# New orders for the compute engines of an attention and gMLP kernel, and a narrower marking product

## The chip, the cores and the metric

The kernel runs on one core of a Trainium2 chip. The core has five instruction queues that matter here: TensorE (PE: matrix products; its weight loads are shown as PEld), VectorE (DVE), ScalarE (ACT), GpSimd (POOL) and SyncE (SP, which issues most DMAs). Each works through its own list of instructions strictly in order and waits on semaphores for the others. The metric is the device time of one execution in microseconds (us): the kernel before has a median of 224.09 over three runs (223.98 to 225.09).

## The reference

Two blocks in sequence, all in bf16, with S = 2048 tokens and D = 512:

```python
# block A: linear attention, 32 heads of 16
q, k, v = split(layernorm(x) @ wqkv)
phi = lambda t: where(t > 0, t + 1, exp(t)) + 1e-6
kv  = einsum('bhsd,bhse->bhde', phi(k), v)
z   = einsum('bhsd->bhd', phi(k))
h   = x + (phi(q) @ kv / (phi(q) . z)) @ wo
# block B: gMLP, 1792 = 2 x 896 hidden columns
z1, z2 = split(gelu(layernorm(h) @ w_in))
g   = w_sp @ layernorm(z2) + b_sp[:, None]    # mixes the 2048 tokens
out = h + (z1 * g) @ w_out
```

(This is a shortened form of it, in the order in which the kernel works. The layer norms have no learned scale.)

## The kernel before

Everything stays on chip between the first load and the last store. Tokens are cut into 16 tiles of 128. PSUM, where PE leaves its products, has eight banks of 512 fp32 columns.

How the program is made. The kernel's code first records operations: an operation is one or several instructions of one engine, with the tiles that it reads and writes. The recorders are short helpers, so many instructions carry the helper's line: PE products L434, ACT L453, DMAs L464 and transposing DMAs L467. Dependences follow from the tiles read and written, those of PSUM by bank. The order of the 1315 operations is not that of the code: a constant, `ORDER` (line 16), holds a packed list of their numbers, which `schedule` (L144) unpacks and deals out to the engines:

```python
ids = np.frombuffer(zlib.decompress(base64.b85decode(ORDER)), np.uint16).tolist()
self.order = {e: [o for o in self.seq if o.eng == e] for e in self.ENGS}
```

`emit` (L163) then puts in the semaphore waits that the dependences ask for. So an order that is another one changes neither what is computed nor what depends on what, but an engine that reaches an instruction too early stands there, with all that is behind it in its list.

The stages, in order of time, with the lines that they show in the profile:

- *0 to 12 us.* Token tiles x are loaded; DVE takes each tile's statistics (L543, gathered by L544), the reciprocal deviation rs is made by ACT for the first tiles (Ln, then Exp) and by POOL later (L549, L551, L556), DVE or ACT normalizes (xn, L588), and PE transposes the first tiles (L602); later ones go through transposing DMAs.
- *8 to 54 us.* PE projects K, then Q (weights wqkv, tokens xnT). phi takes an exponential on ACT (e), one DVE instruction on e (L614), and one that joins it with the product in PSUM: pk for K and pqT for Q (L619, or ACT and DVE L617). PE accumulates ct from pk and xn (L692), then combines it to kvm and m (L790, L794). Meanwhile DVE forms sums of weight tiles that Strassen's method needs later (L755; of w_in: ws, of w_sp: sa, sae, wt).
- *45 to 68 us.* For each of four groups of 512 tokens: PE makes the denominators (L824), ACT takes their logarithm (r) and from it the reciprocal (rcp), four SP DMAs spread rcp over the partitions (L815), DVE multiplies pqT with it (L840). Then PE multiplies pqT with m, four products for a token tile, and DVE adds x and evicts the sum as h (L852). ACT squares h and POOL makes its moments and the power -1/2 (L564 to L583, L575 to L579 for pairs of tiles), DVE normalizes (hn, L588), and SP transposes it by DMA (hnT).
- *66 to 139 us.* The gMLP's input product, in cells of seven Strassen products (`cell3`, L905; operands hnT and hs, weights win and ws): ACT copies between banks, DVE adds partial results (L882). gelu is applied on ACT at eviction (z, z1t). z2's norm: for even tiles ACT squares (sq) and POOL makes moments (L567 to L570) and the power (L583); for odd tiles DVE takes statistics (L952, L953) and POOL the power (L549, L551). DVE then normalizes in place (z<-z,st,rs, L588) and sums tiles (zt).
- *104 to 212 us.* The mixing product over tokens, Strassen again, some of it nested (`mix` L1067, `nested` L1042): operands z, zt, nv; weights wt, sa, nu. ACT adds the bias, DVE gates with z1.
- *172 to 219 us.* The out product, in pairs of token tiles (`mo_pair`, L1159), which use PSUM banks 6 and 7 (the last pair 3 and 4), then DVE adds h and the result is stored.

The marking product. In `mo_pair` all products but the first of each bank add onto what is in the bank. Ahead of that, columns that no starting product has touched must be written once. For bank 7 this is a product 512 columns wide ahead of the loop (L1210); in the loop a product 64 columns wide (L1217) does it for the last pair's bank 4, on columns 448 to 511, without `start`. Both products' values are of no use to the result.

Of the kernel before, what the change touches and what calls it, by code (L numbers as in the profile page):

```python
# [32 lines left out]
class _Prog:  # L33
# [219 lines left out]
def bass_sequential_preLN__linear_attn_block__mixer_gmlp__prompt_kernel(  # L253
# [24 lines left out]
    g = _Prog(nc)  # L278
# [43 lines left out]
    x = g.sbuf("x", o_x, [NT, D], BF16)  # L322
    h = g.sbuf("h", o_x, [NT, D], BF16)
# [6 lines left out]
    hnT = g.sbuf("hnT", o_pk, [KD, S], BF16)  # L330
# [4 lines left out]
    z1 = [g.sbuf(f"z1t{n}", o_xnT + slot[n] * ZR, [FH], BF16) for n in range(NT)]  # L335
# [14 lines left out]
    N4 = HT // 2 * (HW // 2) * 2  # L350
# [65 lines left out]
    def bank(b, n=512, lo=0):  # L416
        return psum[:, b, lo:lo + n]
# [5 lines left out]
    def PE(fn, reads, writes, ns, **k):  # L423
        return g.add("PE", fn, reads, writes, cost=ns, lat=165, **k)
# [372 lines left out]
    for c in range(KD):  # L797
        b = CB[1 - c % 2]
# [18 lines left out]
    for tg in range(NG):  # L817
# [12 lines left out]
        if tg not in MERGE:  # L830
# [135 lines left out]
    lo, hi = slice(0, HW), slice(HW, FH)  # L966
# [227 lines left out]
    for k in range(0, HT, 2):  # L1194
# [5 lines left out]
        if k == 0:  # L1200
# [9 lines left out]
    PE(lambda pe: pe.matmul(bank(7), lhsT=hnT[:, 0, 0:P], rhs=wout[:, 0, :], start=True, stop=True), [hnT[:, 0, 0:P], wout[:, 0, :]],  # L1210
       [bank(7)], 216)
    wout_sums()
    for c, i in enumerate(MIX[:-1]):
        X, Y = (3, 4) if i == MIX[-2] else (6, 7)
        if Y != 7:
            rest, any_, w = psum[:, Y, HW:512], zgT[MIX[0]][:, 0, :], wout[:, 0, 0:512 - HW]
            PE(lambda pe, rest=rest, any_=any_, w=w: pe.matmul(rest, lhsT=any_, rhs=w, start=False, stop=True,  # L1217
                                                               skip_group_check=True), [any_, w], [rest], 65)
        mo_pair(i, c % 2, X, Y)
# [34 lines left out]
```

## Time and profile before

| | before |
|---|---|
| median of three runs | 224.09 us (223.98 to 225.09) |
| profiled execution, span from first to last instruction | 222.3 us |
| PE busy | 216.2 us, 97% |
| DVE busy | 202.8 us, 91% |
| ACT busy | 142.8 us, 64% |
| POOL busy | 47.1 us, 21% |
| granted TensorE clock | 1.000 |

Of the profiled execution the page gives the span; its own time is not told, and the median is 1.8 us above that span. In the rows of the timeline the first number is the start in us, the second the length in us of one or (xN) several instructions together, then engine, line, operation, output and inputs by name with their shapes, and in brackets how long the engine had been idle and who released it. Instructions of one engine overlap at their ends, so the spacing of two starts is often shorter than the length shown: sixteen 512-column products in 3.61 us start some 0.216 us apart.

### The profile page before, as it was taken

The page shows a single profiled execution, that of the slowest core. Times are in us where ns is not written, and L with a number is a line of the kernel's source. Part 1 is how long each engine was busy: PE and PEld are TensorE (multiplying, and loading weights), DVE is VectorE, ACT ScalarE, POOL GpSimd, SP SyncE. Part 2 cuts the span into 40 slices and gives each one's busy share as a digit, 9 for nine tenths or more (in the row PEclk, how much of TensorE's full clock was granted, in tenths as well). Part 3 has the DMA queues.
Part 4 walks back from the last instruction along what each step waited for, and adds up shares of the span by engine and source line. Part 5 has one row for each costly group of instructions (what it writes and reads, how often), then busy time and mean ns, then how long its engine had stood idle before and what let it go on. Part 6 is the DMA issues. An engine that isn't in the chain of part 4 may idle for free.

```text
span 222.3 us, 3865 instructions
## 1 busy us (share of the span) xinstructions
PE 216.2 (97%) x1346; PEld 123.6 (56%) x1346; DVE 202.8 (91%) x472; ACT 142.8 (64%) x283; POOL 47.1 (21%) x133
## 2 busy tenths in 40 slices
PE   7799999999999999999999999999999999999995
PEld 7443444443344444444555556666676787767764
DVE  3899967899999999999989998999999989899995
ACT  5789663299889999999872546626475246732330
POOL 4334410000547554685720000000000000000000
PEclk9999999999999999999999999999999999999999
DMA  6758877928966555304993653995372205033574
GB/s 182 246 99 227 170 180 181 237 50 193 182 137 132 112 107 85 49 0 94 179 134 88 166 116 81 161 202 107 58 152 58 41 0 70 17 88 27 127 203 142
DMA packets 75026, 27.12 MB, mean 122 GB/s; under 512 B 64768, under 2 KB 75008, under 8 KB 75008
## 3 DMA queue, kind: packets, MB, share of 16 engines
q1 hardware_dynamic: 74304, 26.30, 57.0%
q10 hardware_dynamic: 704, 0.59, 0.9%
q8 instruction: 10, 0.16, 0.3%
q14 instruction: 8, 0.07, 0.1%
HBM read 6.95 MB, written 2.10 MB: 41 GB/s over the span
## 4 chain that ended last, share of the span: by engine, by line
PE 87%; DVE 4%; DMA 3%; ACT 3%; SPq 1%; issue 1%; ACTq 0%
PE psum L434 79%; PE psum L692 6%; DMA x<-in_A_x_dram 1%; SPq L815 1%; DMA r<-rcp 1%; ACT e L453 1%; DVE pqT L840 1%; DVE h L852 1%; DVE st L543 1%; DVE pk L619 1%; PE psum L602 0%; PE psum L824 0%; PE psum L714 0%; PE psum L790 0%; DVE e L614 0%
## 5 line engine op out<-in xcount | busy, mean ns | idle before, releaser
L453 ACT ACTIVATE psum<-psum 128x448 f32<-128x448 f32 (+2 forms) x76 | 31.1, 428 | 34.9 <-PE psum L434 28.6
L434 PE MATMUL psum<-z,wt 128*128 128x448 bf16 (+1 forms) x216 | 42.0, 335 | 0.1
L434 PEld LDWEIGHTS psum<-z,wt 128*128 128x128 bf16 x216 | 20.9, 98 | 14.6 <-ACT np L453 0.4
L434 PE MATMUL psum<-win,hnT 128*128 128x448 bf16 x112 | 26.4, 353 | 0.0
L453 ACT ACTIVATE e<-psum 128x1024 bf16<-128x1024 f32 (+1 forms) x18 | 16.7, 929 | 8.5 <-PE psum L434 8.5
L453 ACT ACTIVATE z1t<-psum 128x448 bf16<-128x448 f32 (+1 forms) x24 | 16.4, 691 | 7.3 <-PE psum L434 5.3
L434 PE MATMUL psum<-ws,hs 128*128 128x448 bf16 x72 | 19.2, 353 | 0.0
L434 PEld LDWEIGHTS psum<-win,hnT 128*128 128x128 bf16 x112 | 10.5, 98 | 11.0 <-ACT z1t L453 1.0
L434 PE MATMUL psum<-zt,sa 128*128 128x448 bf16 (+1 forms) x92 | 16.5, 316 | 0.0
L882 DVE TENSOR_TENSOR psum<-psum,p5z 128x448 f32<-128x448 f32 x24 | 15.0, 626 | 1.0 <-ACT z1t L453 0.8
L692 PE MATMUL psum<-pk,xn 128*128 128x512 bf16 x64 | 15.8, 379 | 0.1
L453 ACT ACTIVATE p<-psum,b 128x448 f32<-128x448 f32 x22 | 13.4, 634 | 3.6 <-DVE u L1030 1.8
L434 PE MATMUL psum<-m,pqT 128*128 128x512 bf16 x64 | 14.7, 380 | 0.9 <-DVE h L852 0.6
L434 PE MATMUL psum<-xnT,wqkv 128*128 128x512 bf16 x64 | 15.3, 379 | 0.0
L453 ACT ACTIVATE z<-psum 128x896 bf16<-128x896 f32 x16 | 15.0, 970 | 0.2 <-PE psum L434 0.2
L434 PE MATMUL psum<-wqkv,xnT 128*128 128x512 bf16 x64 | 15.0, 379 | 0.0
L1030 DVE TENSOR_TENSOR u<-psum,p 128x448 bf16<-128x448 f32 x22 | 13.6, 620 | 1.4 <-PE psum L434 1.0
L434 PE MATMUL psum<-wout,zgT 128*128 128x256 bf16 (+1 forms) x77 | 14.9, 302 | 0.0
L434 PE MATMUL psum<-nv,nu 128*128 128x224 bf16 x108 | 14.5, 259 | 0.1
L543 DVE BATCH_NORM_STATS2 st<-x 128x6 f32<-128x512 bf16 x15 | 9.8, 682 | 3.6 <-DMA x<-in_A_x_dram 3.6
L614 DVE TENSOR_SCALAR e<-e 128x1024 bf16<-128x1024 bf16 (+1 forms) x18 | 7.0, 390 | 5.6 <-ACT e L453 5.6
L434 PEld LDWEIGHTS psum<-zt,sa 128*128 128x128 bf16 x92 | 8.9, 98 | 5.3
(157 smaller groups left out, 452.2 us busy)
## 6 DMA issues: line engine op xcount, KB each, us to landing
r<-rcp SPq DMA_DIRECT2D x16, 128.0 KB, 2.7
out_dram<-h SPq DMA_DIRECT2D x15, 128.0 KB, 1.8
win<-in_B_w_in_dram SPq DMA_DIRECT2D x4, 448.0 KB, 3.8
x<-in_A_x_dram SPq DMA_DIRECT2D x6, 256.0 KB, 3.8
wqkv<-in_A_wqkv_dram SPq DMA_DIRECT2D x2, 512.0 KB, 4.9
wout<-in_B_w_out_dram SPq DMA_DIRECT2D x1, 896.0 KB, 5.1
wt<-in_B_w_sp_dram SPq DMA_TRANSPOSE x32, 4.1
wo<-in_A_wo_dram SPq DMA_DIRECT2D x1, 512.0 KB, 6.4
```

What stands on the lines that cost most here:

```text
L434: inst = pe.matmul(out_ap, lhsT=a, rhs=b, start=start and i == 0, stop=stop and i == len(pairs) - 1, **kw)
L453: return g.add("ACT", lambda ac: ac.activation(out_ap, in_ap, func, **kw), [in_ap, *extra], [out_ap] + ([accum] if accum is not None else []),
L543: dve(lambda v: v.bn_stats(s[:, 0:6], src[:, n, :]), [src[:, n, :]], [s[:, 0:6]], D)
L614: dve(lambda v: v.tensor_scalar(e, e, 1.0, EPS_PHI, op0=ALU.min, op1=ALU.add), [e], [e], w * GW, acc=4)
L619: dve(lambda v: v.scalar_tensor_tensor(dst, t, 1.0 + EPS_PHI, e, op0=ALU.add, op1=ALU.max), [t, e], [dst], w * GW, ps=True)
L692: inst = pe.matmul(bank(CB[c]), lhsT=xn[:, i, c * P:(c + 1) * P], rhs=pk[:, i, :], start=i == 0, stop=i == NT - 1)
L815: g.add("SP", lambda q: q.dma_start(dst, src_ap), [rcp[:, i:i + w, :]], [dst], cost=700, lat=2200, dma=f"r{tg}{c // 2}")
L840: dve(lambda v, q=q, r=r: v.tensor_tensor(q, q, r, ALU.mult), [q, r], [q], 2 * GW, acc=2)
L852: dve(lambda v, n=n, b=b, s=s: v.scalar_tensor_tensor(h[:, n, :], bank(b), 1.0, x[:, n, :], op0=ALU.mult, op1=ALU.add, accum_out=s[:, 0:1] ...
L882: dve(lambda v: v.tensor_tensor(half(b), half(src), p, ALU.add), [half(src), p], [half(b)], HW, ps=True)
L1030: dve(lambda v: v.tensor_tensor(u, half(b), p, ALU.add), [half(b), p], [u], HW, ps=True)
```

## The change

Two things. First, `ORDER` holds another list. The list of SP is the same as before, instruction by instruction, and so is the order of the DMAs that ACT issues. Of the other engines' operations this many stand at another place of their engine's list:

| engine | operations | at another place | farthest move |
|---|---|---|---|
| PE | 349 | 208 | 15 places |
| DVE | 456 | 380 | 94 |
| ACT | 255 | 160 | |
| POOL | 129 | 87 | |

The moves that the prediction speaks of, with the place in the engine's list before and after:

| engine | operation | before | after |
|---|---|---|---|
| DVE | statistics of x tile 2 | 4 | 2 |
| PE | tile 0's K projection and tile 1's transposes | | change places |
| DVE | statistics of an x tile at 20 us, ahead of e and pk | 44 | 41 |
| ACT | at 46 us: e, then r of the first token group | e, r | r, e |
| DVE | eviction of h, tile 1 | 93 | 90 |
| DVE | a norm of h (hn) | 110 | 107 |
| PE | products of pqT and m, two pairs at 54 to 68 us | | change places |
| DVE | a sum of w_in tiles (ws, at 46.45 us before) | 74 | 131 |
| DVE | sums of w_sp tiles (wt, wt, sa) | 129, 120, 153 | 187, 214, 223 |
| DVE | norms of z2, tiles 0 to 3 | 159, 164, 171, 169 | 141, 155, 165, 173 |
| DVE | norms of z2, tiles 4 to 7 | 176, 180, 185, 178 | 162, 170, 177, 172 |
| POOL | power of z2's tile 0 | behind tile 2's moments | ahead of them |
| POOL | power of z2's tile 4 | behind the start of tile 6's moments | ahead of it |
| ACT | squares of z2 tiles 8 and 10 | 111, 118 | 118, 122 |

Second, bank 7's marking product: the one 512 columns wide goes, and the loop's 64-column product is now made for bank 7 too, in the first turn. It reads the first tile of zgT and wout, and stands in PE's list two products ahead of the first product into bank 7.

```diff
-ORDER = "c-jrsg92EG76ibvyXVHXZM%(a+qN4!jcwbuZQHgR+kEdQX3Qd3M1#e%kQT`zTPO=_AuOClv8Wc>qF
...
+ORDER = "c-jrsg92EG76ibvyXVHXZQE&V+qP}nwr!hjY@2Ot+sS+L6BE(QA{Z>5g|d)Fi)@iBtcA0v7RAC_T
...
-    PE(lambda pe: pe.matmul(bank(7), lhsT=hnT[:, 0, 0:P], rhs=wout[:, 0, :], start=True, stop=True), [hnT[:, 0, 0:P], wout[:, 0, :]],
-       [bank(7)], 216)
     wout_sums()
     for c, i in enumerate(MIX[:-1]):
         X, Y = (3, 4) if i == MIX[-2] else (6, 7)
-        if Y != 7:
+        if c == 0 or Y != 7:
             rest, any_, w = psum[:, Y, HW:512], zgT[MIX[0]][:, 0, :], wout[:, 0, 0:512 - HW]
             PE(lambda pe, rest=rest, any_=any_, w=w: pe.matmul(rest, lhsT=any_, rhs=w, start=False, stop=True,
                                                                skip_group_check=True), [any_, w], [rest], 65)
         mo_pair(i, c % 2, X, Y)
```

More of the change, by code (lines that the diff above doesn't have):

```diff
@@ L15 @@
 SEM_NS = 45.0
-ORDER = "c-jrsg92EG76ibvyXVHXZM%(a+qN4!jcwbuZQHgR+kEdQX3Qd3M1#e%kQT`zTPO=_AuOClv8Wc>qFG!EZ()okbBk|*C9&w1z;at6OK3?grzN&zmdA2gDobv8EuW>f6jsPmS{lo5g)OZWup*Yu3R(=yVCgNU)v;n0%Q9Il%VHU=u4T5`*4FA-QLArREt|ErzpS`5vg}sU8e1D{XF05bwYPt)ft9urR?!+-U+Z8Ut&^3ps#ePSS!}Che_LlOYhA3rRkmvOuT`-D*3|}DIje3HZLl@9I5x<J*?7BQO>Brwvf)<4CRj}?Z<DQ=O|hXi&AM50n`$j=x^=giw#Zsq51VC6td%Xb#n#hi*fJYwy==LSuoZU8R@y4tWxZ{Wjk49Y+xA)?+h=QRwC%UqHpbT40Xt}iY>qv#n>N<w+F@H~M{J(WxAk_^#@PnjiUqdOHrY12ZCmY;J-3Cn-5%R9+hIHHxLvdBw%JbDe|FBE*-1NVr)-Ozw@bDS7wm<dw##<k&e#=uYCCb!Lg15qw2-)JpY4@>u$Xvfp+LN}SO7vJ3}WMp3Gt8!@$uCnBQfH@5g;ypSQ31*DEMwE@Y7NwIieyV{#a7{vT!g&M>0f1SUj)<_-!$e2Dy<6X;Bt=5FQzj5=D>>c@Y8WQ32%;5&4i2`B4-FP#*Uz5(=UYilHL1pg0PlKI$SX3Zn!{A~RYe8%iM)D&cRmLj%;qU#N^WsDhqoh#aVjYAB5@$d2}Cgg&T_GU$cjXpDc*7i}>LwU7(7(E*2%6JOB;M=$~%u?zpA6Q-dlYM?WEV>G&8CTe0oMq)aeVJXI77VcO-%)kot$1)7SYz#zm9K~2HM|XTf3yi}`%)ubs!vTE99lW<5IDxr1hOYR5L%5HY=!U!aiIZ4`*Y*&<&<dxp8jmm@$1wp1@c<KX8bk3IZ|oAD;1vdA9<uW?hG0I<U=3bl0j^*Ya_}mK;WyS|3f^EH{@^b<jc2hP<Tb3vTf`^$H?KoHhpC9mw-zuY6YvHWBPZi=GD7h`B;p2y<~xL7E+*zvB;<K4#506p628YG+(cwPM{agwQbu7KZo~&vR#--5ccx`DF2N>*V>;$xU0y(5_F#TS=VlaSc&6t?^yCY~U?F})ZD!yt6ksprV;z1%M%H5y-bQ^UV^KC>VP;})He@j-XJ+<cITmLGenulkWK8bhOEhMAreG_^;=kO^5{%8(tiUYn%bkqGHXO(=NXd%a#Z=77ww%jK?9Y-M#5gR)*&M)j+|4=c$0i)Y_8iQiT)=ru&G~G~1Kh)5T*%UF#&OKX;cU)D+=2Hj!?#?_@m$5qoWOUyYsdKyS92meup^i716%N+P2vcyVM~7GWPavueBwwRW)&{wT2^H>e&Ifh;uNmqRDS1Zp5QW0<5za#L9XXse&ZOP<PR?A3ZCKyj^!`@<VKd|5pLpdPUj)6<Z13_bwZo@hi7>1|Mc#~3{stWlr<;?a^2^7hR_y<)Ha@FD0Sg6&SYp^WIEkr6@^hvhSeor;8xycI9=v7hSw}U;uTicRX$)Ob!7xS=0ir*9$aT+)#43C(Gx~fRNdr%jIO7wqpFIfTa2M+yv>-Zr8|tRnu?>i+Q)h-sCatLgo>}6ddURJr9{fB#LB0nN}?C6uU9OpWGbeHdd&t(uHt&bluDu8YNQfMrIJdoLQ11js;wf*q|$1v!b+|3%C9CWqY65q?5e9uYN`Tip|V=4f0R)zl}ByVUagf?9aK)u)LE0&T$xovUDQ!iv|Jg~Nz>KVE2^t{sG7QIn!2l%dTN0F)=IVWHJYJp8mND~zxrvWX6d`;Xtidmx7KQ|)~THasjYr!yf$dC)@!5s=!k}>msaVh7HX(QsDp3PFm2W%4Od?s)>ci`NS)Nb+M;Eer)?Ug(ORN|`b+bbR^j}VCTN$&=(iT=tj21wj%%DIYP$|;w|1zL?^O=%R7XFppW3HCdaN_bqU##zdlcT!>4yH(Bpp*EKd)4NNf&feceFy6wO<!?Kv(tT|7G72{H}f}vR~12MfENo-DCPa(L1}my}wX2cfY2mx~*9LQh~?u2;S9WdmF#6DBjIOcz5sN!#%Et^amQ@J$=6S@)#b<M|p3L=lQ*lztX?n*ZX^X590$pu@CZop2QRQ0w3V1J)w{GAwI^3`Wub)<UZcVc`^^}6aAqkcqxCRbUw+`dm_){lf9}Z^(p>LQ$3@<)oV@nus+Rac?zH5GrfS%@wvX;7y4p<r$xTR)A)NW^_0Hcmw5*Ntd;&jJAH+x^~}D?cX%d0?`yr9XYtj3!6SMO&*|$utFQ4*UfTciY@Xe7d39gs1%0D$@W1_|F8Xf&q%FS3w|XJZ>wA5$@Aopk&$sz5Kj?-1fS2_zI^>r;pFi`XUe1quO+V#_{iN6OuR7wFy|$P4V_wH|`w6e$SG<PT^D}<d>v|C{=JoxB7xk<D+^_j{Z|uXoxZm^!-o#6K3BTbDy`nesTi)Coc?<uh+kV$8`5nLSoBf_w_A1`gANfOn;30yR{@7pnYiBUqTm3)skiiq5=W&AnJXD~dwZHK&LFnL}hYQ~NX%8C&!3Pf?y!3Pa-aUvE#0{SMM~@Ih3E~A2gD)OE_~y}qPyWLr2Qh-r9yR#s@q?JbFOL;`^#noe;JYUZ{&>RRw<iuPND}-H1t^N4"
@@ new lines @@
+ORDER = "c-jrsg92EG76ibvyXVHXZQE&V+qP}nwr!hjY@2Ot+sS+L6BE(QA{Z>5g|d)Fi)@iBtcA0v7RAC_T#IHhx4`0C5{quREvY52yq3@sSu)FG$t|(vv;3CIQdkK4%TiiuD`07?u!XjQmeyie5es7(ET$E;x)#d{Svsq2#Vx(nvpUwsGFg4gXbmijWwv%!%(7WlYiv2Ky_K@I*2EfG2g`0HtfS?yidNDZSsCkO{jHL9wk}rM%33uWXq7Ftm9t#d)w)>~8)VgOfK|1@HpIGHd8=WQY?w8(p*F?h*hs5sH?64+x2ZPSYS}a!Wz(&KHMix~(`MKRn`td<j`gsXHrIODQfp<)>>rzDt!;(vvz6A{X4@EBWqoY4t+v~?#`fA;>uZ18SX*cN?SS>O^)}At+d&&|hiro#wRv{fZrKETZVT*)O|*r!(T>?7+hjYi*f!e^``5PEL)&RvZHeu&NA}o`+itsVCv1=1ux)nI?%8%bW#{d*?ZG*FYA@`vU9gvS#;({!J8M_%nq9Jx_+%d~Cf?Zx3xUt}#A1PXW}yJYMreF7Aq?Un5#r;kMMh%8fg=gNSzHA8VNvkiQsAfkvgC-0)JTXwmK0$T9fo8GhiLe132@)iAO`Xx71E+8!XqCtpd3;n9rB|X(jy`&;x9x%0c1pZ)I~uQ!d;7m3Mh;$D2{q)fFj6>5~zfdXpd~jgi@%CTxf_ksE;bhjGQQqMre!PsEQoej>hPKYUqdTsE#tIfj(%5Q7DW4Xo9{tf~KgAv1o=oIEp%Gj*h5_6ZneU7=TXLi*eYAnHY%97>)7hf)%KRL70Ux7>qeMfFYQTmFSB9tQ%HiE>>XzzM%!?VIq2>C5GZ4j^R7j;4bFlBo1Q%j-wa;LwBsjPn^OX9Kt%BMi0EUdsvSLn1nO<fmT?EhggKxxR1#gfnRupw>AZrF$|CK3L9_*!;zgEF&$^|%B~^@Ut=V$;T(Qr6W(Adaxy-R=dlaU>sXApApam2Z{PyN8Muheh|2^7Lo(nc<YqjE;xs%#BHqM1gl1yqVF*4&LN3EIEI}A1;dA6=WWK;syhjfv<t;?vZKUA`Y(aj8WmKkRPv&DZhU33T$K?pmt*FOdjKIHGh!Gi`1(=?FxD7E_kQrEq^;wiL8Ht4%i$$1`v00bBnT*BQkS|f3eVK`kn3?67h5guoCD@q#`4O!dhsoK5yZ8wen3XA5k)M&0yP1lW*oH$mfP2`Ml{tv1*^UcXg@1D}2eK;XaUrv@8i#Wz_i{elvm_UD1c$K$5Aq+5WGOCTbx!0cF5(xI=2GrP8NTN-mgO5;%OmW_No>kH)`^|Dj>|ck%{ZA4tU0@IJzH=EPjCvyupGzoZ){)<j^lVv<y)TQN*>}yw&Z@i<20_~2d?G>PUlDN<0j7FXU=3Re&SJX=3%bk79QXiZsja~<u)GUckaVCZs&Ra;Bo%sFLvcU{^o4Hx0?Jzs5VXKSc}wIp5X=Vpp;I5y3=)+rx`-0IG2}LMIjYh7a2;I*^LhwMspZe;dF)98D3X;hxd7nRTV*zw389_4<7LbBkLv~Fq$4Sif-`<qv|Q6tA=7Img*{|p0SW_Gq(O^9R0_*dd~War`k%WYKpJ@e90F~p!`atzm!<Hl~hSoOAYjj#gt6N)lje5NXeB)CG>_Vl|p&dSS6K8rIcQ2R9Hn+T6I)ZnN&tiR6rHfRP|I=sZ~+UlwBQESuIsgC$&NyHOe!pmCCEFMteRrS0}YmR<-ql>Z%s1q-n~m)~c!M>ZZ;bs0?baRT``{+NkyFu2~wSPCnMBYmBedY<2NoYVUKERz1{CU364EwOPY-Oj|TWoqeW;tG9A#j{0bW`YM}7Xr0z-zWQmNhH9j?YP1&UghpwbW@wW7YrDp1fEMbMHffP|=(v_Br*>+bmTIw<E1WM=cptC5`l(%7t-p0x6SP}Lv`62yUq5tO|LBp<=&|-`tS0M*ChCyRDUzR64&78&Kd<P1P?7zBvS^B)=s!jE=ZfZ0{Dpq$mLm9X-BC=B<#+W*FLmMnnZMFyT~s^2r`R6HZ!48w(Iv(67!IE*d0fAytBUU(oPJ%2-TkTlRX6YMNxY+{_E6r#pDBSS^Pb+vdwD_+JdyYIwEji~yszI^8c*&IG{7I~tp<5NU*t)>zc2Q59>QO1sHgCO9@+={5KrmpJ*1EG+&;p``*44+T|U9X`XtZbOFg4c^eMi?KWnmQ^4&hwGy4~PP#DkR-!#o<cr~Byvpk>Y@ajI(=Xyk+?Q=Y<*YssR-?RC0U*H9Og|GBgp552@JFWJdp35(I9xvk`Rmk)EC$06;zQJqwCST{ne2W+My}sTrdRf2hfB9D5=tX?9|LxoTAK&5Se4p?1{eHmr_#rRq2R*OX^74MzYx`Fn@j8CYD|lT$;Ya<MSM+**%Io_jKklc!fuHm%Ud+$>RX^v&{hD9*k^bCocoQ$-H~p43^-^Ba8~Sap<juX2xA4Z^(*O0!e#igwd;Zd!c~#%$5B#n_^!r}LLj;e!mA~@WKF<*_Sm=*EWS}5U(Aq-<PrQu>!5a?~gbu<5?>ua9#^3q}_aJ<5-rxHRj~he^KKfIS5JU;$1rdWU9zFQx(SlF@!y^YVg3tcbqXzMVSivuk8GQ8wLG0kWCkp;}!r-?j4lGC#{0}I;ilG"
```

## The prediction

> **What bounds the kernel now.** I read the page from the top: span and busy times, the chain of work that ended last, then PE's waits.
>
> ```profile
> span 222.3 us, 3865 instructions
> ...
> PE 216.2 (97%) x1346; PEld 123.6 (56%) x1346; DVE 202.8 (91%) x472; ACT 142.8 (64%) x283; POOL 47.1 (21%) x133
> ...
> PE 87%; DVE 4%; DMA 3%; ACT 3%; SPq 1%; issue 1%; ACTq 0%
> ```
>
> TensorE (PE) is the bound: 97% busy, and 87% of the chain. No PE product goes but one, so a new order can win only time in which PE stands still. The waits of PE name who holds it (us in all, times, longest):
>
> ```profile
> PE psum L602 <- DVE xn L588: 1.2, 2, 0.9
> PE psum L626 <- POOL warm L471: 1.0, 1, 1.0
> PE psum L434 <- DVE h L852: 0.6, 2, 0.4
> PE psum L434 <- DVE pqT L840: 0.2, 1, 0.2
> ```
>
> It is VectorE (DVE) nearly every time. Where, the table by stage shows (stretch, length, then busy us of PE, weight loads, DVE, ACT, POOL; granted clock; DMA share; GB/s):
>
> ```profile
> 54.40:68.00 13.60, 12.76 (x60) 5.24 (x61) 12.74 (x33) 11.86 (x27) 6.45 (x22) 1.00 0.78 159
> 68.00:104.00 36.00, 35.95 (x187) 16.92 (x185) 35.91 (x87) 35.19 (x71) 22.55 (x53) 1.00 0.42 77
> ...
> 139.00:176.00 37.00, 36.94 (x268) 25.69 (x268) 35.69 (x86) 19.13 (x45) 0.00 (x0) 1.00 0.61 114
> ```
>
> The clock is full throughout. From 54 to 68 us PE stands visibly (12.76 of 13.60); from 68 to 104 DVE and ACT are as full as PE; from 139 on PE has no gap, so what is done there can only lose. An estimate of what there is to win after the first 7 us, from the spacing of PE's products against their count: 0.3 at 22, 1.7 from 54 to 68, 0.7 from 68 to 104 and 0.7 from 131 to 139, in all some 3.4 us.
>
> **The change, step by step.** SP's list, and with it every DMA's place in its queue, stays as it was, and so do the DMAs that ACT issues; the lists of PE, DVE, ACT and POOL change. "Place" is the place in an engine's list.
>
> *1. Head.* DVE takes the statistics of x tile 2 (place 4 to 2) into its wait for tile 1's data; PE does tile 0's K projection before tile 1's transposes.
>
> ```profile
> 4.50 1.29 DVE L543 BATCH_NORM_STATS2 st<-x 128x6 f32<-128x512 bf16 x2 [0.43 <-DMA x<-in_A_x_dram]
> ...
> 7.08 1.04 PE L602 MATMUL psum<-ident,xn 128*128 128x128 bf16 x12 [0.32 <-DVE xn L588]
> 7.52 0.47 SPq L464 DMA_DIRECT2D wqkv<-in_A_wqkv_dram  x1
> ...
> 12.16 0.43 PEld L434 LDWEIGHTS psum<-xnT,wqkv 128*128 128x128 bf16 x3 [0.22 <-DMA wqkv<-in_A_wqkv_dram]
> ```
>
> PE's first products come up to 0.43 + 0.32 = 0.75 us sooner. But at 12.16 the first Q projection waits for a weight whose load was issued at 7.52 behind other loads on SP, which no compute order moves. What is won before stands there again: bounds 0 and -0.75; I take -0.05, near the wait that remains.
>
> *2. At 20 us.* A statistics instruction (half of the 1.29 above, 0.64 us) goes ahead of DVE's e and pk.
>
> ```profile
> 20.44 0.46 DVE L614 TENSOR_SCALAR e<-e 128x1024 bf16<-128x1024 bf16 x1 [0.31 <-ACT e L453]
> 20.93 1.23 DVE L619 SCALAR_TENSOR_TENSOR pk<-psum,e 128x1024 bf16<-128x1024 f32 x1
> ...
> 20.19 1.90 PE L434 MATMUL psum<-wqkv,xnT 128*128 128x512 bf16 x8
> 22.21 1.04 PE L692 MATMUL psum<-pk,xn 128*128 128x512 bf16 x4
> ```
>
> DVE idles 0.31 there, so the instruction costs at most 0.64 - 0.31 = 0.33 on the chain to 22.21, and nothing if the statistics' tile allows it to start while DVE waits. It starts when pqT before it ends, near the start of that idle time: bounds 0 and +0.33, taken +0.05, since the two PE products swapped there (places 21 and 22) give PE other work meanwhile.
>
> *3. At 46 us.* ACT does the first token group's logarithm r ahead of the exponential e, which before came first.
>
> ```profile
> 46.19 1.06 ACT L453 ACTIVATE e<-psum 128x1024 bf16<-128x1024 f32 x1
> 47.10 0.72 ACT L453 ACTIVATE r<-psum,epst 128x512 f32<-128x512 f32 x1
> ...
> 47.74 1.23 DVE L619 SCALAR_TENSOR_TENSOR pqT<-psum,e 128x1024 bf16<-128x1024 f32 x1
> ...
> 49.27 1.04 PE L434 MATMUL psum<-xnT,wqkv 128*128 128x512 bf16 x4
> ...
> 51.64 1.02 ACT L453 ACTIVATE e<-psum 128x1024 bf16<-128x1024 f32 x1 [0.27 <-PE psum L434]
> ```
>
> e, DVE's e and pqT slip by 0.72; pqT ended at 48.97 and PE's product that overwrites its bank came at 49.27, a slack of 0.30. So PE waits 0.72 - 0.30, about +0.4, and nothing behind takes it back: the next e, at 51.64, waits for PE. Bounds 0 (DVE, relieved of one 0.6 us sum, still starts no sooner than e) and +0.72.
>
> *4. From 54 to 68 us.* DVE evicts tile 1's h three places sooner (93 to 90), a hidden-layer norm goes from 110 to 107, and two pairs of PE's attention-out products are swapped.
>
> ```profile
> 54.41 3.61 PE L434 MATMUL psum<-m,pqT 128*128 128x512 bf16 x16
> 58.39 1.04 PE L434 MATMUL psum<-m,pqT 128*128 128x512 bf16 x4 [0.37 <-DVE h L852]
> ...
> 62.70 3.63 PE L434 MATMUL psum<-m,pqT 128*128 128x512 bf16 x16 [0.25 <-DVE h L852]
> 61.18 3.54 SPq L815 DMA_DIRECT2D r<-rcp  x4
> 66.93 0.69 DVE L840 TENSOR_TENSOR pqT<-pqT,r 128x1024 bf16<-128x1024 bf16 x1 [0.60 <-DMA r<-rcp]
> 67.68 1.04 PE L434 MATMUL psum<-m,pqT 128*128 128x512 bf16 x4 [0.23 <-DVE pqT L840]
> ```
>
> Sixteen products from 54.41 at 0.216 each end at 57.87; the next began at 58.39, so 0.52 us were lost to the eviction, which the move covers. The stall at 62.70 (0.25) may go with the swaps. But late next is the chain at the end: four r transfers, 3.54 us of issuing that SP does in order, then the landing and DVE's multiply at 66.93, and PE waits for it. That chain begins with PE's denominators behind the product of 58.39, so it moves ahead with the 0.52 and no further. Bounds 0 and -1.4 (the stage's 1.7 less what stands before 54.41); I take -0.6, the covered stall and a little.
>
> *5. From 68 to 104 us.* Three sums are put off past this stretch (places 129 to 187, 120 to 214, 153 to 223) and one out of step 3's; the norms of z2's tiles are pulled ahead: tile 0 from place 159 to 141, tile 6 from 185 to 177; POOL does tile 0's power straight after its moments.
>
> ```profile
> 45.85 0.69 DVE L755 TENSOR_TENSOR sae<-wt 128x1024 bf16<-128x1024 bf16 x1
> 46.45 0.62 DVE L755 TENSOR_TENSOR ws<-win 128x896 bf16<-128x896 bf16 x1
> ...
> 80.83 0.31 POOL L569 TENSOR_SCALAR st<-st 128x1 f32<-128x1 f32 x1
> ...
> 93.02 0.26 POOL L567 TENSOR_SCALAR st<-st 128x1 f32<-128x1 f32 x1 [1.37 <-ACT sq L453]
> 97.21 0.89 POOL L570 TENSOR_SCALAR st<-st 128x1 f32<-128x1 f32 x1
> 98.19 0.68 POOL L583 TENSOR_TENSOR rs<-st,expo 128x1 f32<-128x1 f32 x1
> ...
> 96.93 1.08 DVE L755 TENSOR_TENSOR zt<-z 128x1792 bf16<-128x1792 bf16 x1
> 101.23 0.50 DVE L588 TENSOR_SCALAR z<-z,st,rs 128x896 bf16<-128x896 bf16 x1
> ```
>
> A sum takes 0.60 (45.85 to 46.45), so by 102 us DVE is some two sums (the third comes in exchange for a statistics pass), 1.1 us, ahead. Against it: tile 0's norm now stands some 7 us sooner, and its power can end at about 80.83 + 0.31 and two short POOL steps (0.24 and 0.64, estimated), 82.1, when DVE is there about 0.4 sooner and stands. Tile 6's norm is reached at 96.93 (eight places sooner), and its power ended at 98.87; POOL fills its 1.37 of idling before 93.02 with the steps moved there, and if the 0.89 at 97.21 takes the usual 0.24, the power ends near 98.87 - 1.37 - 0.65 = 96.9. So of the 1.1 us some 0.7 remain up to that norm, and nothing behind it; only the stage's 0.7 us of PE stalls can be bought with it, and I take half, -0.3. Bounds: -0.7, and 98.87 - 96.93 = +1.9 if POOL comes no sooner.
>
> One page bears on POOL's share of that. The row of one POOL step (times, then least, median and largest ns):
>
> ```profile
> L570 POOL TENSOR_SCALAR st<-st x10: 225/240/1065, 5.9 to 108.9; 128x1 f32<-128x1 f32 x10
> ```
>
> Nine of ten alike and one four times as long: something holds POOL at times. The Trainium skill, page "SBUF — State Buffer", section "SBUF: two separate sides", says that VectorE and GpSimd share a pair of ports, as an exclusive lock held for a whole instruction. By that rule DVE's two-input sums beside POOL's chain lengthen it as the new order happens to pair them, and the sum would go from gain to loss, as rival C works out from the row; the long one agrees with it, no run here isolates it.
>
> *6. After 104 us.* PE's, DVE's and ACT's orders change in places, among work that has no gap before (36.94 of 37.00). The put-off sums come back here, about 0.5 us of DVE more ahead late on; DVE's free 1.3 of 37 us cover it. Taken 0; bounds 0 and +0.5. The 0.7 us at 131 to 139 is a chain of sums and products whose order stays.
>
> *7. The marking product.* In the chain's rows (start, us):
>
> ```profile
> 176.12 0.21 PE psum L1210
> ...
> 212.07 0.03 PE psum L1217
> ```
>
> The wide product goes, a second narrow one comes, on the gapless part: 0.03 - 0.21 = -0.18. It reads zgT's first tile, which an output product uses some 4 us before, so no wait is added.
>
> Sum: -0.05 + 0.05 + 0.4 - 0.6 - 0.3 + 0 - 0.18 = -0.68. The profiled execution is known by its span, 222.3, which would become 221.6; 1.8 us lie between it and the median of 224.09, taken as unchanged: 223.4.
>
> **Rivals.** A, the relief carries through: step 3 stays hidden because denominators move ahead too (0), step 4 yields its whole 1.4, step 5 half: -1.4 - 0.35 - 0.18 = -1.9, 222.2. For it: DVE ends nearly every wait of PE. Against: SP's 3.54 us of issues stay in order.
>
> B, slower, POOL's powers: DVE works in order, so a norm reached before its power holds up every eviction behind it, in a stretch where DVE has 0.09 us free of 36. If tile 6's power ends at 98.87 as before, step 5 is +1.9 in place of -0.3: -0.68 + 2.2 = +1.5, 225.6. It decides where POOL gains less than the 1.1 us that DVE gains. For it: POOL began the tile's moments only when ACT's square let it (1.37). Against: the steps now ahead fill that wait.
>
> C, slower, POOL's steps stretch: two of tile 6's four steps at 1.065 in place of 0.24 add 1.65 us to its chain: -0.68 + 1.65 = +1.0, 225.1. For it the one long step, against it nine short ones. This is what the Trainium skill's rule cited in step 5 would do here.
>
> D, the order does nothing: the weight's landing, SP's r chain and the sums at 137 us are fixed, gains and losses cancel, and the marking alone remains: 223.9.
>
> **How the numbers follow.** About 0.5%, 1.1 us, is what this kernel's measurement can tell from no change. Forecast 0.40 and D 0.08 lie within it (its own range 223.0 to 224.3); A 0.26 is faster; B 0.17 and C 0.09 slower. The time is the forecast's, 223.4. The range takes in A and C and stops just short of B's 225.6: 221.9 to 225.5.
>
> **What would show it.** PE's wait for h at 58 us gone; a new PE wait of 0.4 us near 49; the last r multiply still waiting for its DMA; DVE idle before L588 of z2 by under 0.5 us; no 0.21 us product at L1210. Wrong it is if DVE stands a microsecond or more for POOL at a z2 norm, if PE gets gaps after 139 us, or if the stage from 54 to 68 loses its stalls whole.

## The result and the profile after

The changed kernel is slower: 225.72 us median (225.0 to 226.34) against 224.06 us, a ratio of 1.0061 (95% interval 1.004 to 1.0082), where 223.4 was forecast, with 221.9 to 225.5 as the range. A second measurement, on the chip of the first experiments, gave 225.33 against 224.05, 1.0062 (1.0042 to 1.0081). (The ratio is not the quotient of the two medians, which is 1.0074; the means of the runs, 225.63 and 224.28, give 1.0060.) The profiled execution took 225.64 us, with a span of 223.8, which is 1.5 longer than before.

The page and the waits of PE after the change (us in all, times, longest):

```profile
span 223.8 us, 3856 instructions
...
PE 216.4 (97%) x1346; PEld 122.9 (55%) x1346; DVE 203.7 (91%) x472; ACT 143.3 (64%) x283; POOL 48.6 (22%) x133
...
PE 72%; DMA 8%; DVE 7%; ACT 6%; POOL 3%; issue 1%; SPq 1%; ACTq 0%; POOLq 0%
```

```profile
PE psum L434 <- DVE pqT L840: 0.5, 1, 0.5
...
PE psum L434 <- DVE z L588: 0.4, 1, 0.4
PE psum L434 <- DVE psum L882: 0.3, 1, 0.3
```

PE is as busy as it was, in a longer span, and POOL, which was in no place of the chain, now holds 3% of it. The wait for h that was the largest of the attention stage is gone; behind the head two new ones have come, for z2's norm (L588) and for a partial sum in PSUM (L882). One stretch of the table by stage, before and then after (columns as in the prediction's table):

```profile
106.00:116.00 10.00, 10.00 (x55) 5.11 (x53) 9.33 (x23) 8.24 (x17) 4.79 (x12) 1.00 1.18 165
```

```profile
106.00:116.00 10.00, 9.26 (x49) 4.45 (x48) 9.43 (x22) 6.18 (x13) 5.89 (x15) 1.00 1.08 166
```

Between 106 and 116 us PE was without a gap before (10.00 of 10.00); now it stands, and gets 49 products done in place of 55.

A ledger makes this exact. PE's products follow each other at fixed spacings (512 columns 0.216 us; eight of 448 columns start to start 1.51). I summed these along each kernel's own list and took the sum from the starts: what remains is the time that PE has stood by then. The table gives, by stage, how much more or less a kernel's PE stands than that of the kernel before (us; the last stage includes the shorter marking product). The kernels below "changed" are those of the experiments, described further down; "(before +)" marks the ones made from the kernel before, the others are made from the changed kernel.

| kernel | to 26 | 26-51 | 51-72 | 72-106 | 106-116 | 116-143 | 143-end | sum |
|---|---|---|---|---|---|---|---|---|
| changed, first | +0.60 | +0.31 | -0.30 | -0.39 | +1.09 | +0.20 | -0.01 | +1.49 |
| changed, second | +0.21 | +0.32 | -0.31 | -0.40 | +1.09 | +0.20 | 0.00 | +1.11 |
| squares_back | -0.20 | +0.32 | -0.31 | 0.00 | +0.24 | +0.20 | -0.02 | +0.23 |
| square8_back | +0.02 | +0.32 | -0.31 | 0.00 | +0.24 | +0.20 | -0.02 | +0.43 |
| wt8_later | +0.43 | +0.32 | -0.31 | -0.40 | +0.74 | +0.36 | -0.01 | +1.13 |
| squares_wt8 | -0.14 | +0.32 | -0.31 | 0.00 | +0.08 | +0.36 | -0.01 | +0.29 |
| hn_back | +0.42 | +0.32 | -0.10 | -0.40 | +1.10 | +0.20 | 0.00 | +1.53 |
| exp_first | -0.51 | 0.00 | -0.38 | -0.40 | +1.09 | +0.20 | 0.00 | 0.00 |
| square8_exp | +0.63 | 0.00 | -0.03 | 0.00 | +0.24 | +0.20 | -0.01 | +1.03 |
| squares_off (before +) | +0.66 | 0.00 | -0.74 | -0.14 | +2.05 | +0.01 | +0.01 | +1.84 |
| sums_off (before +) | +1.08 | +0.22 | -0.87 | +0.40 | +0.41 | +0.36 | 0.00 | +1.59 |
| stage54_mark (before +) | +0.31 | 0.00 | +0.20 | -0.02 | 0.00 | 0.00 | -0.19 | +0.30 |
| mark_only (before +) | +0.31 | 0.00 | 0.00 | 0.00 | 0.00 | 0.00 | -0.18 | +0.13 |

The two executions of the changed kernel agree to 0.01 us in every stage but the first, where loads land, and differ there by 0.4. So a stage behind 26 us can be read to a few hundredths, and the head can not. The one great loss stands at 106 to 116 us: +1.09, twice the other losses behind the head (0.31 and 0.20), and more than the gains (0.30 and 0.39).

The square of z2's tile 8 on ACT and the start of that tile's moments on POOL, before:

```profile
95.32 1.04 ACT L453 ACTIVATE sq<-z 128x896 bf16<-128x896 bf16 x1
```

```profile
98.96 0.55 POOL L567 TENSOR_SCALAR st<-st 128x1 f32<-128x1 f32 x1
```

and after:

```profile
100.64 0.98 ACT L453 ACTIVATE sq<-z 128x896 bf16<-128x896 bf16 x1
```

```profile
101.80 0.27 POOL L567 TENSOR_SCALAR st<-st 128x1 f32<-128x1 f32 x1 [1.35 <-ACT sq L453]
```

What happens from there on, read in the chain of waits of the changed kernel (start, length in us):

```profile
100.75 0.96 ACT sq L453 x2
...
101.80 0.28 POOL st L567
102.14 0.55 POOL rs L551
...
102.78 1.44 POOL st L569
...
104.60 0.57 POOL rs L583
...
105.52 0.56 POOL rs L551
106.10 0.51 DVE z L588
...
111.47 0.59 POOL rs L551
...
113.06 0.52 DVE z L588
113.63 1.50 PE psum L434 x7
```

and in its timeline, DVE and PE:

```profile
102.43 1.08 DVE L755 TENSOR_TENSOR zt<-z 128x1792 bf16<-128x1792 bf16 x1
103.43 0.69 DVE L755 TENSOR_TENSOR wt<-wt,wt 128x1024 bf16<-128x1024 bf16 x1
...
106.10 0.51 DVE L588 TENSOR_SCALAR z<-z,st,rs 128x896 bf16<-128x896 bf16 x1 [0.29 <-POOL rs L551]
...
111.58 0.63 DVE L882 TENSOR_TENSOR psum<-psum,p5z 128x448 f32<-128x448 f32 x1
...
113.06 0.51 DVE L588 TENSOR_SCALAR z<-z,st,rs 128x896 bf16<-128x896 bf16 x1 [0.44 <-POOL rs L551]
```

```profile
112.26 0.55 PE L434 MATMUL psum<-win,hs 128*128 128x448 bf16 x2 [0.31 <-DVE psum L882]
...
113.63 1.69 PE L434 MATMUL psum<-z,wt 128*128 128x448 bf16 x8 [0.43 <-DVE z L588]
```

ACT's square of z2's tile 8, put off in the new order (start 95.32 before, 100.64 now), lets POOL begin that tile's moments only at 101.80 (98.96 before). From there POOL, which works in order, has no break until its last power ends at 113.02. The powers of odd tiles stand in the same list: tile 11's (105.52) comes right behind tile 8's (104.60), tile 15's is the last. DVE reaches the norms of these two ahead of their powers and stands 0.29 and 0.44 us, with all that is queued behind; PE waits for the partial sum and the norm that come late. That the late square is the cause is tested below.

### The profile page after: what moved, and what is told of

Its sections match the earlier page's. It is cut to its first block, busy times and chain, and to the rows that moved or that the text cites. A ratio compares the mean times of both kernels' runs of the same rounds, so it can differ in the third digit from the quotient of the medians.

```text
span 223.8 us, 3856 instructions
## 1 busy us (share of the span) xinstructions
PE 216.4 (97%) x1346; PEld 122.9 (55%) x1346; DVE 203.7 (91%) x472; ACT 143.3 (64%) x283; POOL 48.6 (22%) x133
## 4 chain that ended last, share of the span: by engine, by line
PE 72%; DMA 8%; DVE 7%; ACT 6%; POOL 3%; issue 1%; SPq 1%; ACTq 0%; POOLq 0%
PE psum L434 67%; PE psum L692 5%; DMA wqkv<-in_A_wqkv_dram 5%; DMA xnT<-xn 2%; DVE z L588 1%; DMA r<-rcp 1%; DVE st L952 1%; ACT e L453 1%; SPq L815 1%; POOL st L569 1%; ACT ct L453 1%; DVE h L852 1%; ACT z L453 1%; POOL rs L551 1%; POOL rs L583 1%
## 5 line engine op out<-in xcount | busy, mean ns | idle before, releaser
L453 ACT ACTIVATE psum<-psum 128x224 f32<-128x224 f32 (+2 forms) x76 | 31.5, 425 | 33.3 <-PE psum L434 25.1
L434 PE MATMUL psum<-z,wt 128*128 128x448 bf16 (+1 forms) x216 | 41.2, 335 | 0.6 <-DVE z L588 0.4
L434 PE MATMUL psum<-ws,hs 128*128 128x448 bf16 x72 | 18.7, 353 | 0.0
L882 DVE TENSOR_TENSOR psum<-psum,p5z 128x448 f32<-128x448 f32 x24 | 14.9, 624 | 0.3 <-ACT z1t L453 0.2
L434 PE MATMUL psum<-nv,nu 128*128 128x224 bf16 x108 | 13.8, 259 | 0.1
```

What stands on the lines that cost most here:

```text
L434: inst = pe.matmul(out_ap, lhsT=a, rhs=b, start=start and i == 0, stop=stop and i == len(pairs) - 1, **kw)
L453: return g.add("ACT", lambda ac: ac.activation(out_ap, in_ap, func, **kw), [in_ap, *extra], [out_ap] + ([accum] if accum is not None else []),
L882: dve(lambda v: v.tensor_tensor(half(b), half(src), p, ALU.add), [half(src), p], [half(b)], HW, ps=True)
```

## The experiments

**The changed kernel again.** No edit.

> The changed kernel once more, as a control on the chip of the next three. If the loss is in the order, PE has again some 1.07 us of gaps at 112 to 114 us, in front of the cell product that waits for L882 and of the mixing product that waits for the norm L588 of z2, and the time stands some 1.5 us above the kernel before. If the 0.36 us that the first Q projection came later (12.64 against 12.28) was the spread of DMA landings and not the order, that figure differs by 0.2 us or more from the first profile; if it is the order, it stays within 0.1.

The gaps of 1.09 us came back to the hundredth, at 225.33. For the head this run alone decides nothing: the first Q projection started at 12.50 in place of 12.64, and 0.14 lies between the two limits that were set. Over the fourteen profiled executions it started between 11.82 and 12.64, by 12.11 to 12.47 with the head of before and 11.82 to 12.64 with the new one. With one and the same order it spreads by 0.8 us, so the 0.36 us between the first two profiles is not shown to be the order's.

**squares_back.**

```diff
 ACT, changed kernel
   z (gelu) of tile 8, z of tile 10
+  square of tile 8
   ... four evictions of the input product's cells
-  square of tile 8
+  square of tile 10
   z1t, z, z
-  square of tile 10
```

> The changed kernel, with ACT's squares of z2 tiles 8 and 10 back at their places of before (ahead of the four evictions, and behind the last of them). Theory S (POOL starts the moments of tile 8 only at 101.80 because the square comes 5.3 us later than before, and is busy without a break from there to 113.0): POOL's step starts near 99.8, its last power ends some 1 us sooner, PE's gaps at 112 to 114 shrink from 1.07 to 0.4 or less, against up to 0.4 us of new gaps at 97 to 104 from the later evictions: 225.2. Theory W (what counts is the two DVE sums back to back, zt and wt, that hold up a POOL step for 1.43 us and delay DVE itself): the gaps stay above 0.8, 225.6.

224.54 us, 1.0023 (1.0009 to 1.0037), below the 225.2 that was expected: by the time more than half of the loss is gone with two of ACT's instructions, by the ledger behind the head about half (+0.90 to +0.43). What the two profiles differ in besides lies in the head (+0.21 and -0.20), which the edit does not touch. POOL's timeline:

```profile
100.12 0.27 POOL L567 TENSOR_SCALAR st<-st 128x1 f32<-128x1 f32 x1
...
101.10 0.30 POOL L569 TENSOR_SCALAR st<-st 128x1 f32<-128x1 f32 x1
```

The moments start at 100.12, and the step that took 1.43 us takes 0.30. The gaps at 106 to 116 fall from +1.09 to +0.24; what the put-off square had won at 72 to 106 (0.40) is given back in full. Theory S holds for the gaps.

**wt8_later**, and **squares_wt8**, which adds it to squares_back.

```diff
 DVE, changed kernel
   zt sum (102.43)
-  wt sum (103.43)
   ...
   last norm of z2 (113.06)
+  wt sum
```

> The changed kernel, with the wt sum that stands at DVE's place 187, at 103.43 us, put behind the last norm of z2, so that it no longer follows the zt sum of 1.09 us. Theory W: the POOL step L569 that took 1.43 us ends with the zt sum, so takes 0.9 or less, DVE and POOL are 0.6 us sooner at the last norms, and PE's gaps at 112 to 114 shrink from 1.07 to some 0.3: 225.0. Theory S: POOL still starts tile 8's moments at 101.8, and the gaps stay above 0.8: 225.6.

> Both edits together, the squares back and the wt sum later. If both causes add, PE's gaps at 112 to 114 are gone (under 0.2 us) and the time is 224.6 to 224.9; if one of them is the whole cause, the time equals that of the one that helps alone. If neither is, it stays at 225.7.

225.27 (1.0052), between what the two theories gave, and 224.68 (1.0024). In wt8_later the POOL step becomes shorter, as theory W has it, and ends with the sum that is left:

```profile
102.25 1.08 DVE L755 TENSOR_TENSOR zt<-z 128x1792 bf16<-128x1792 bf16 x1
```

```profile
102.59 0.91 POOL L569 TENSOR_SCALAR st<-st 128x1 f32<-128x1 f32 x1
```

1.43 us with two sums beside it, 0.91 with one, 0.30 with none. But on PE this wins 0.35 at 106 to 116, and 0.16 is lost again behind, where the sum now stands. With the squares back the same edit moves 0.16 from 106 to 116 us to the next stage (0.24 to 0.08, then 0.20 to 0.36) and wins nothing. So W is real and small.

**square8_back.** As squares_back, with tile 10's square left where the change put it.

```diff
 ACT, changed kernel
   z (gelu) of tile 8, z of tile 10
+  square of tile 8
   ... four evictions
-  square of tile 8
```

> The changed kernel, with ACT's square of z2 tile 8 alone back at its place of before; that of tile 10 stays put off. If it is tile 8's square that POOL stands for (idle 1.35 us before that tile's moments) and tile 10's finds POOL busy anyway, PE's gaps at 112 to 114 fall from 1.07 to 0.4 or less as with both back, while half of the 0.4 us won at 97 to 104 is kept: 224.3 to 224.6. If both squares count, the gaps stay above 0.6: 224.9 or more.

224.66 (1.0025, 1.0012 to 1.0038), and the ledger is that of squares_back in every stage behind the head. Tile 8's square is the whole of it, on both sides of the account: I had expected to keep half of the 0.40 won before, and none was kept.

**squares_off.** The kernel before, with nothing but the two squares put off.

```diff
 ACT, kernel before
   z of tile 8, z of tile 10
-  square of tile 8
   ... evictions, psum<-psum
-  square of tile 10
+  square of tile 8
   p5z, z1t, z, z
+  square of tile 10
```

> The kernel before, with one thing of the change alone: ACT's squares of z2 tiles 8 and 10 put off to their new neighbours (behind the four evictions, and behind the next gelu). Theory S (late squares make POOL late, and DVE stands at a z2 norm): POOL's moments of tile 8 start some 1.5 us later than their 98.96, those of tile 10 some 3 us later, PE gets gaps of 0.8 us or more at 106 to 114, against up to 0.3 us won at 97 to 104: 224.6 to 225.6. If the squares hurt only together with the new order of POOL and DVE, the gaps stay under 0.3 and the time is 223.8 to 224.1.

225.89 against 223.91, 1.0098 (1.0072 to 1.0124): above what was expected, and more than the whole change costs. POOL, DVE and PE there:

```profile
100.97 0.27 POOL L567 TENSOR_SCALAR st<-st 128x1 f32<-128x1 f32 x1 [2.20 <-ACT sq L453]
...
104.83 0.27 POOL L567 TENSOR_SCALAR st<-st 128x1 f32<-128x1 f32 x1 [3.02 <-ACT sq L453]
```

```profile
108.06 0.51 DVE L588 TENSOR_SCALAR z<-z,st,rs 128x896 bf16<-128x896 bf16 x1 [1.42 <-POOL rs L583]
```

```profile
110.29 0.55 PE L434 MATMUL psum<-ws,hs 128*128 128x448 bf16 x2 [1.38 <-DVE psum L882]
```

In the order of before POOL takes tile 8's and tile 10's moments early, so it stands 2.20 and 3.02 us for them, DVE stands 1.42 at the norm, PE 1.38 behind DVE. The late squares suffice by themselves. With the new order of POOL and DVE they cost less (1.09 in the change, 2.05 here); which of its moves does that was not tested.

**sums_off.** The kernel before, with the four DVE sums alone at their new places.

```diff
 DVE, kernel before (places)
-  74 ws,  129 wt,  120 wt,  153 sa
+ 131 ws,  187 wt,  214 wt,  221 sa
```

> The kernel before, with the four DVE sums alone (one of w_in, three of w_sp) put off to the places that they have in the changed kernel, 0.5 to 1.7 us less of DVE work ahead from 46 to 104 us. If DVE's relief buys PE's gaps from 68 to 104 us, as the prediction's step 5 has it, they fall by 0.3 from 0.7 us and the time is 223.6; if it buys nothing, the gaps stay and the time is 223.9 to 224.1; if the sums come late for the mixing products, PE has new gaps at 110 to 140 us and the time is 224.3 or more.

225.31, 1.005 (1.0034 to 1.0066). From 72 to 106 us PE stands 0.40 us longer, not less, and from 106 to 143 us 0.77 longer: the time of the third case, with a loss from 72 to 106 us that none of the three had. The first new gap of that stage, where the sum of w_in now goes ahead of the sums of hn:

```profile
79.94 0.54 PE L434 MATMUL psum<-ws,hnT 128*128 128x448 bf16 x2
80.61 0.55 PE L434 MATMUL psum<-ws,hs 128*128 128x448 bf16 x2
```

Two products of 448 columns take 0.38 us, and 0.67 passed. The w_in sum had stood at 46 us beside a DVE that waited for ACT anyway, and was moved into the stage in which DVE is full. What the three sums of w_sp do there without it was not tested.

**hn_back.** The changed kernel, with DVE's first norm of h behind two more evictions, as before.

```diff
 DVE, changed kernel
-  94 hn, tile 0
   h, h
+  96 hn, tile 0
```

> The changed kernel, with the first norm of h (hn, tile 0) at DVE's place 96 as before in place of 94, behind two more evictions of h. If DVE's stand of 0.47 us there (its power on POOL ended at 60.16) is what makes PE wait 0.69 us at 63.70 for the multiply with r, that gap shrinks to 0.3 or less: 0.4 us faster than the changed kernel, 224.9 to 225.2. If the r chain is the limit all the same, the gap stays and the time is that of the changed kernel.

225.52, 1.0068 (1.005 to 1.0086): no gain. In the changed kernel DVE stood at that norm, and PE behind the multiply:

```profile
60.20 0.41 DVE L588 TENSOR_SCALAR hn<-h,st,rs 128x512 bf16<-128x512 bf16 x1 [0.47 <-POOL rs L583]
```

```profile
63.70 2.76 PE L434 MATMUL psum<-m,pqT 128*128 128x512 bf16 x12 [0.53 <-DVE pqT L840]
```

With the norm back the first stall shrinks and another appears at the end of the r chain:

```profile
63.05 2.76 PE L434 MATMUL psum<-m,pqT 128*128 128x512 bf16 x12 [0.35 <-DVE pqT L840]
...
68.69 1.47 PE L434 MATMUL psum<-m,pqT 128*128 128x512 bf16 x6 [0.51 <-DVE pqT L840]
```

```profile
66.57 0.69 DVE L840 TENSOR_TENSOR pqT<-pqT,r 128x1024 bf16<-128x1024 bf16 x1 [0.49 <-DMA r<-rcp]
```

So with the norm back the four r transfers become the limit, which in the changed kernel they were not: there the last multiply with r, at 67.58, followed without a wait. The reason stands in SP's list, where tile 0's transposed norm (hnT) is directly ahead of these transfers. In the changed kernel and then with the norm back:

```profile
60.64 1.19 SPq L467 DMA_TRANSPOSE hnT<-hn  x1
61.87 2.88 SPq L815 DMA_DIRECT2D r<-rcp  x4
```

```profile
61.20 1.19 SPq L467 DMA_TRANSPOSE hnT<-hn  x1
62.44 3.24 SPq L815 DMA_DIRECT2D r<-rcp  x4
```

A norm that DVE does 0.57 us later holds back SP, and with it r, by the same 0.57, though rcp itself was done at 61.54.

**exp_first** (the changed kernel with ACT's e ahead of r at 46 us again) and **square8_exp** (that and square8_back).

```diff
 ACT, changed kernel, 46 us
-  r, e, rcp
+  e, r, rcp
```

> The changed kernel, with ACT's exponential e ahead of the logarithm r at 46 us, as before. If that swap is what makes PE wait 0.20 us at 50.19, the wait goes, the later r costs nothing, and the time is 0.2 to 0.3 us shorter: 225.1 to 225.4. If the sooner r was needed, the multiply with r at 54 us waits for its DMA, up to 0.4 us, and the time is that of the changed kernel or above.

> The changed kernel with tile 8's square back and the exponential e ahead of r at 46 us. If the two losses are separate, the gains add (0.8 and 0.4): 223.9 to 224.2, level with the kernel before. If the stage from 54 to 68 takes one of them back, 224.4 or more.

224.93 (1.0043, 1.0027 to 1.0058), a little under its expectation, and 224.68 (1.0017, 1.0002 to 1.0032), within the second case that was expected. The +0.31 of 26 to 51 us goes, as expected; but DVE now waits for r's transfer and PE behind it:

```profile
51.71 0.69 DVE L840 TENSOR_TENSOR pqT<-pqT,r 128x1024 bf16<-128x1024 bf16 x1 [0.26 <-DMA r<-rcp]
```

```profile
54.00 2.33 PE L434 MATMUL psum<-m,pqT 128*128 128x512 bf16 x10 [0.30 <-DVE pqT L840]
```

The stage 51 to 72 then stood at -0.38 in one and -0.03 in the other, so from 26 to 72 the swap is worth 0.39 in one and 0.04 in the other: unclear. That stage moves even where its order is the same (0 in mark_only, -0.74 in squares_off, both with the order of before there): SP took 3.45 us to issue the last four r transfers in the one and 2.64 in the other.

**stage54_mark** (the kernel before, the new order between 54 and 69 us alone, and the narrow marking product) and **mark_only** (the narrow product alone).

```diff
-    PE(lambda pe: pe.matmul(bank(7), lhsT=hnT[:, 0, 0:P], rhs=wout[:, 0, :], start=True, stop=True), ...
-        if Y != 7:
+        if c == 0 or Y != 7:
```

> The kernel before, with the changed kernel's relative order of PE, DVE, ACT and POOL between 54 and 69 us alone, and the narrow marking product. If that stage's order is the one part of the new orders that wins by itself (some 0.35 us of PE's gaps there, beside 0.16 for the marking), the time is 223.4 to 223.6, under both kernels; if the r chain takes it back, 223.8.

> The kernel before, with its order, and the narrow marking product at the place of the wide one. PE's spacing there goes from 0.216 to some 0.05 us, and as nothing else moves the time falls by 0.16 us: 223.9. If a wait shows up in its place (zgT or the bank), the fall is less than 0.1.

224.46 against 224.16 (1.0017, 1.0006 to 1.0029): above both cases that were expected; the stage's order wins nothing by itself (+0.20 in the ledger). mark_only took 223.84 against 223.91, 1.0001 (0.9982 to 1.0021): the product itself is as cheap as worked out, and the sum too small for the time to show.

```profile
176.27 0.19 PE L1215 MATMUL psum<-wout,zgT 128*128 128x64 bf16 x1
176.29 1.68 PE L434 MATMUL psum<-zt,wt 128*128 128x448 bf16 x8
```

No kernel here is faster than the kernel before beyond its interval.

## Why the prediction was wrong

Step by step, with the ledger's numbers (predicted, then measured):

- Step 1, the head: -0.05; no difference that stands out of the landing of loads, which spreads PE's standing up to 26 us from -0.51 to +1.08. Not contradicted, and the greatest noise of this kernel.
- Step 2, 20 us: +0.05; the gap at pk was 0.43 in two pieces before and 0.41 in one after. Right.
- Step 3, r ahead of e: +0.4; +0.31, with the wait where it was placed (PE at 50.19 for pqT L619). The mechanism right and the size nearly so. Whether the sooner r wins part of it back at 54 us stays unclear (exp_first and square8_exp).
- Step 4, 54 to 68 us: -0.6; -0.30. The covered stall went, but the r chain was not the limit that the step took it for. PE stood longest behind a multiply that DVE reached late (0.53 at 63.70), after 0.47 us at a norm of h that was moved from place 96 to 94 and not looked at; that norm also sets when SP comes to the r transfers (hn_back).
- Step 5, 68 to 104 us: -0.3; -0.39, right by number and wrong by reason. DVE's relief bought nothing on balance: with the squares back nothing of the 0.39 is left (squares_back), and the four sums by themselves cost 0.40 (sums_off). What won it was ACT: the put-off square let four evictions through sooner. That the number came out near is luck. The row of L570 was also misread: it gives the least, the median and the largest of ten, not nine alike. In the trace of before six of the ten take some 0.23 us, two some 0.4, one 1.065 and one the 0.89 at 97.21 that the step itself shows.
- Step 6, after 104 us: 0, with +0.5 as the upper end; +1.09 at 106 to 116, +0.20 up to 143 and +0.15 behind it (the table's -0.01 holds the marking's -0.16). **This is the step that failed.** It took the order to change "among work that has no gap before" and let DVE's free time cover it. PE had no gap there, but POOL's list had no room for a late input. The two squares of z2's tiles 8 and 10 stood in the table of moves, and I gave them no price and followed nobody who waits for them. The row that rival B quotes, POOL standing 1.37 us for a square, showed the link. They were to be followed as the z2 norms of tiles 0 to 7 were: square, moments, power, norm, product.
- Step 7, the marking: -0.18; -0.16 (0.216 before, 0.058 after with the wait at its start). Right.

The measured steps add up to +0.9 us, beside the head's spread: a slower kernel, as it came out. Tile 8's square is half of that (+0.85 at 106 to 116, -0.40 before); of the 0.24 that is left at 106 to 116 the wt sum makes 0.16, which only moves to the next stage. Rival B named the mechanism, a DVE that reaches a norm ahead of its power and holds up everything behind, and its price (+1.5 in all) is near the result by luck: it laid it on the norms of tiles 0 and 6 that were pulled ahead, and DVE stands at neither. It was an earlier link of the same chain, in a later tile, that had been put off. Rival C's stretching happened, in one step of tile 8 in place of two of tile 6 (1.43 for 0.30 us), and cost PE at most 0.35.

Most signs that the prediction named for itself came true (no wait for h, the wait near 49 us, DVE under 0.5 us at the z2 norms), and the kernel is slower all the same. DVE's two stands, 0.29 and 0.44 us, each stayed under the microsecond that was to show an error, while PE lost 1.09 in that stretch.

Left open: the +0.20 at 116 to 143 us, which every kernel with the new order has (of those with the old one only sums_off loses there, 0.36, by its own sums), and the +0.15 at the end. The spacings say where they lie. The first is the chain of sums and products near 139 us, of which step 6 said that its order stays: DVE's order of the nu sums does change there, and PE stands 0.50 between 137 and 141 us where it stood 0.29. Of the second some 0.12 is PE's longer stand behind the last marking product, at 213.3 us. None of the runs puts these orders back, so the causes are not shown.

## What to carry to other kernels

When an order is changed, follow each instruction that is put off to its last consumer, not only those that are pulled ahead: an engine that is 22% busy (POOL here) can set the end if its input comes late and its own list allows no other work. A gap-free stage is no cover: PE has no slack there to take up a delay that arrives from an earlier one. And put what a move wins in one stage beside what it costs in the next: the same square won 0.40 us and cost 0.85.

## What the runs showed of the hardware

A POOL step of 0.30 us took 1.43 us while DVE ran two sums of two SBUF tiles back to back, 0.91 with one, and ended 0.09 and 0.17 us behind the last of them. The 1.43 came back at 1.43 to 1.44 in the three other executions that pair them so (after_again, hn_back, exp_first). Lengths on POOL are rough, but its next step started accordingly, at 104.29 and 103.59. The Trainium skill, page "SBUF — State Buffer", section "SBUF: two separate sides", has VectorE and GpSimd share a port pair as a lock for a whole instruction; the trace agrees in kind, and shows more than that sentence says: POOL did not get in between the two sums, though each is an instruction of its own.

And the spread of this kernel's time is mostly in its first 26 us. PE's standing there differed by up to 1.6 us over the fourteen profiled executions, and by 1.1 among those with the new order of the head. The first Q projection, which waits for a weight's landing, moved by 0.8 of it; what moved the rest was not followed. Meanwhile every later stage but that of the r transfers repeated to 0.02 us between kernels with the same order there.
